# Cosine attention into a GELU feed-forward: two score passes move in front of w_in, and the norms' roots move to GpSimd

## The chip, the cores and the metric

The kernel runs on one core of a Trainium2 chip. The metric is the device time of one execution in microseconds (us). The engines of the core run side by side, each through its own queue of instructions, and wait for each other by semaphores: TensorE (PE; PEld is its weight load), VectorE (DVE), ScalarE (ACT), GpSimd (POOL) and SyncE (SP), which here only issues transfers.

## The reference

Attention over normalised q and k (8 batches, 12 heads, 448 rows, head size 64), then a feed-forward block with an exact GELU (768 to 2048 to 768).

```python
q_n = q / (np.linalg.norm(q, axis=-1, keepdims=True) + 1e-06)
k_n = k / (np.linalg.norm(k, axis=-1, keepdims=True) + 1e-06)
scores = np.matmul(q_n, k_n.transpose(0, 1, 3, 2)) / tau
attn = softmax(scores)                          # written out, with 1e-09 in the divisor
x = np.matmul(attn, v)                          # (8, 12, 448, 64), then to (3584, 768)
h = x @ w_in
g = 0.5 * h * (1.0 + erf(h / sqrt(2)))
out = g @ w_out
```

## The kernel before

Four heads make a quad; a batch has three (NQ = 3) and the kernel 24. For a quad, GpSimd squares q and k, VectorE sums the squares, a root and a reciprocal follow, GpSimd scales q and k into bf16, and a transposing transfer puts the head size on the partitions. A *pass* is the scores of one of the C = 7 chunks of keys for the four heads: four matmuls on quarter tiles (64x64) into a pair of PSUM banks (`st`), and one exponential on ScalarE that empties the pair. There are three pairs, 0 to 2, and two single banks (`mm0`, `mm1`) that everything else takes in turn. The names in the profile: `st` scores, `pt` their exponentials, `sm` row sums, `o` values, `x` normalised attention, `hp` x times w_in, `g` its GELU, `op` g times w_out, `ot` what is stored.

The norms, with the root as the exponential of half a logarithm on ScalarE (`n` counts groups of one or two quads; units 0 and 1 are the halves of quad 0, so unit u is quad u - 1 after that):

```python
groups = [[n] for n in range(NQ + 2)] + [[NQ + 2, NQ + 3]]
for n in range(2 * NQ + 1, NU, NQ):
    groups += [[n, n + 1], [n + 2]]
...
def logs(n):
    nq = nq_t.pop(n)
    ln_t[n] = nrm.tile(list(nq.shape), F32, tag="lq", name=f"lq{n}")
    nc.scalar.activation(ln_t[n], nq, AF.Ln, bias=tiny)

def roots(n):
    ...                                          # n <= NQ: another layout, same operation
        nc.scalar.activation(sr_t[n], ln, AF.Exp, scale=0.5)

def inverses(n):
    ...
        nc.gpsimd.tensor_scalar(se, sr, 1e-6, None, ALU.add)
    rn = nrm.tile(shape, F32, tag="rn", name=f"rn{n}")
    nc.vector.reciprocal(rn, se)
    rn_t[n] = rn

def root(n):
    logs(n)
    roots(n)
    inverses(n)
```

`both` is what follows the scores of a quad. `upto(f, n)` calls a step for all units below n that it was not called for yet, so it fixes where the step stands in the queues.

```python
def both(g, p):
    sums(g)          # TensorE: row sums, 16 matmuls on 128x32 tiles, in the single bank that is next
    turned(g)        # VectorE: 32x32 transposes of the sums, their sum, reciprocal, spread back
    inverted(g)
    spread(g, 0)
    spread(g, 1)
    values(g, p=p)   # TensorE: 28 matmuls on 64x64 tiles into pair p
    normalise(g, 0)  # VectorE: into x
    normalise(g, 1)
```

Attention of batch b from 1 on. `fill` holds the w_out matmuls of the batches before, 96 or 128 of them, and `run` takes the next share. After each 16th matmul of an output tile VectorE copies the single bank out to `ot`.

```python
group_pairs = [(0, 1, 2), (0, 1, 2), (0, 1, 2), (1, 2), (1, 2, 0), (1, 2, 0), (2, 0), (2, 0)]

def attention(b, fill):
    plan = {96: (20, 13, 13, 12, 16, 22), 128: (24, 18, 20, 18, 22, 26)}[len(fill)]
    ...
    g0, nu = b * NQ, (b + 1) * NQ + 1
    run()
    for n in (nu - 1, nu):
        upto(scale, n)
        upto(transposes, n)
    group(b, 1)
    upto(square, nu + 1)
    run()
    group(b, 2)
    both(g0, 0)
    upto(load_v, b + 3)
    if b == 1:
        upto(load_qk, g0 + NQ + 2)
    group(b, 3)
    upto(square, nu + 2)
    run()
    group(b, 4)
    upto(reduce, nu + 1)
    upto(load_qk, g0 + NQ + 3)
    run()
    group(b, 5)
    both(g0 + 1, 1)
    group(b, 6)
    run()
    group(b, 7)
    upto(reduce, nu + 2)
    n = 2 * b + 4
    if n < len(groups):
        logs(n)
        roots(n)
    run()
    both(g0 + 2, 1)
    if n < len(groups):
        inverses(n)
        done[root] = n + 1
```

The w_in stage: `ahead` blocks of 128 columns get the first four of their six matmuls before the last two chunks of x are there.

```python
def first(b):
    nc.scalar.preload_act_table_set(GELU_SET)
    pairs = (0, 2) if b else (0, 2, 6, 8)
    ahead = 4 if b else 5
    for m in range(ahead):
        bank(m)
        mm(m, range(KD - 2))
    ...                                          # scale, transposes, loads, square, reduce
    for m in range(ahead):
        mm(m, range(KD - 2, KD))
    for m in range(KF):
        if b == 0 and m == 8:
            for i in range(2):
                transposes(4, i)                 # on TensorE, through the single banks
                copies(4, i)
        ...                                      # matmuls of later blocks
        nc.scalar.activation(g_t[sb][:, m, hf * S:(hf + 1) * S], hps.pop(m), AF.Gelu)
        if b == 0 and m == 5:
            nc.scalar.preload_act_table_set(EXP_SET)
            upto(root, 6)
            nc.scalar.preload_act_table_set(GELU_SET)
            upto(scale, nu + 2)
            upto(transposes, nu + 2)
            upto(load_qk, 2 * NQ + 1)
    if b + 1 < B:
        nc.scalar.preload_act_table_set(EXP_SET)
        group(b + 1, 0)
        upto(root, 2 * b + 6)
```

Of the kernel before, what the change touches and what calls it, by code (L numbers as in the profile page):

```python
# [9 lines left out]
F32 = mybir.dt.float32  # L10
BF16 = mybir.dt.bfloat16
AF = mybir.ActivationFunctionType
ALU = mybir.AluOpType
# [3 lines left out]
def kernel(  # L17
# [17 lines left out]
    nc = tc.nc  # L35
    B, H, S, D = q.shape
    C = S // D
    NQ = H // 4
# [9 lines left out]
    consts = ctx.enter_context(tc.tile_pool(name="consts", bufs=1))  # L48
# [4 lines left out]
    nrm = ctx.enter_context(tc.tile_pool(name="nrm", bufs=3))  # L53
# [27 lines left out]
    nc.vector.memset(ones2[64:128, :, 1], 1.0)  # L81
    tiny = consts.tile([128, 1], F32)
    nc.vector.memset(tiny, 1e-30)
    blank = consts.tile([128, S], BF16)
    nc.vector.memset(blank, 0.0)

    root2 = [consts.tile([128, 4 * C, 2], F32, name=f"root2_{n}") for n in range(2)]
# [6 lines left out]
    EXP_SET = "natural_log_exp_and_others"  # L94
    GELU_SET = "gelu_and_others"
# [9 lines left out]
    def pair(i, name):  # L105
        pool = third[0] if i == 2 else ps_st
        return pool.tile([128, 2, 512], F32, tag=f"st{i}", name=name)
# [3 lines left out]

    units = [(0, 0, 1), (0, 1, 2)] + [(g, 0, 2) for g in range(1, NG)]
    NU = len(units)
    groups = [[n] for n in range(NQ + 2)] + [[NQ + 2, NQ + 3]]
    for n in range(2 * NQ + 1, NU, NQ):
        groups += [[n, n + 1], [n + 2]]
    shapes = [[len(gr), 2, units[gr[0]][2] - units[gr[0]][1], C] for gr in groups]
    place = {u: (n, j) for n, gr in enumerate(groups) for j, u in enumerate(gr)}
    qk_t, v_t, sq_t, nq_t, rn_t, qkb_t, qkT_t, pt_t = {}, {}, {}, {}, {}, {}, {}, {}
# [47 lines left out]
    ln_t, sr_t = {}, {}  # L167
# [5 lines that stand above are left out]

    def roots(n):
        ln = ln_t.pop(n)
        if n <= NQ:
            sr_t[n] = root2[n % len(root2)][:, :math.prod(shapes[n])]
            nc.scalar.activation(sr_t[n][:, :, 0], ln.rearrange("p j i s c -> p (j i s c)"), AF.Exp, scale=0.5)  # L178
        else:
            sr_t[n] = nrm.tile(list(ln.shape), F32, tag="sr", name=f"sr{n}")  # L180
            nc.scalar.activation(sr_t[n], ln, AF.Exp, scale=0.5)  # L181

    def inverses(n):
        sr = sr_t.pop(n)
        shape = [128] + shapes[n]
        se = nrm.tile(shape, F32, tag="se", name=f"se{n}")
        if n <= NQ:
            nc.vector.tensor_reduce(se.rearrange("p j i s c -> p (j i s c)"), sr, mybir.AxisListType.X, ALU.add)
        else:
            nc.gpsimd.tensor_scalar(se, sr, 1e-6, None, ALU.add)  # L190
        rn = nrm.tile(shape, F32, tag="rn", name=f"rn{n}")
        nc.vector.reciprocal(rn, se)  # L192
        rn_t[n] = rn

    def root(n):
        logs(n)
        roots(n)
        inverses(n)

    def scale(u, parts=None):  # L200
# [94 lines left out]
    def turned(g):  # L295
        tr = rcp.tile([128, NB, 32], F32, tag="tr", name=f"tr{g}")
        nc.vector.transpose(tr.rearrange("p b r -> p (b r)"), bank_t.pop((g, "sm"))[:, :S])  # L297
        bank_t[g, "tr"] = tr.rearrange("p b (k r) -> p k b r", k=2)
# [22 lines left out]
    def normalise(g, h):  # L321
        b, n = divmod(g, NQ)
        nc.vector.tensor_tensor(x_t[b][:, 2 * n + h, :], bank_t.pop((g, h))[:, :S], rs_t.pop((g, h)), ALU.mult)  # L323

    def both(g, p):
        sums(g)
        turned(g)
# [3 lines that stand above are left out]
        values(g, p=p)  # L331
        normalise(g, 0)
        normalise(g, 1)
# [60 lines left out]
    def upto(f, n, last=None):  # L394
        last = {load_qk: NG, load_v: NV, root: len(groups), load_wi: 4, load_wo: 4}.get(f, NU)
        while done.get(f, 0) < min(n, last):
            done[f] = done.get(f, 0) + 1
            f(done[f] - 1)
# [6 lines left out]
    def attention_first():  # L405
# [148 lines left out]
        sums(2, (6,))  # L554
        values(2, (1,))
        normalise(1, 1)
        logs(4)
        values(2, (2,))
        roots(4)
        values(2, (3,))  # L560
        turned(2)
        inverted(2)
# [9 lines left out]
        done.update({square: 6, reduce: 5, root: 5, scale: 5, transposes: 5})  # L572


    passes = [(n, c) for n in range(NQ) for c in range(C)]
    group_pairs = [(0, 1, 2), (0, 1, 2), (0, 1, 2), (1, 2), (1, 2, 0), (1, 2, 0), (2, 0), (2, 0)]

    def group(b, k):
        n0 = sum(len(p) for p in group_pairs[:k])
        for p, (n, c) in zip(group_pairs[k], passes[n0:]):  # L580
            scores(b * NQ + n, ((0, c), (1, c)), p)
            exps(b * NQ + n, ((0, c), (1, c)))

    def attention(b, fill):
        fill = list(fill)
        plan = {96: (20, 13, 13, 12, 16, 22), 128: (24, 18, 20, 18, 22, 26)}[len(fill)]
        parts = iter(plan)

        def run():
            for _ in range(next(parts)):  # L590
                fill.pop(0)()

        x_t[b] = xp.tile([128, KD, S], BF16, tag="x", name=f"x{b}")
        g0, nu = b * NQ, (b + 1) * NQ + 1
        run()
        for n in (nu - 1, nu):
            upto(scale, n)
            upto(transposes, n)
        group(b, 1)
        upto(square, nu + 1)  # L600
        run()
        group(b, 2)
        both(g0, 0)
        upto(load_v, b + 3)
        if b == 1:
            upto(load_qk, g0 + NQ + 2)
        group(b, 3)
        upto(square, nu + 2)
        run()
        group(b, 4)  # L610
        upto(reduce, nu + 1)
        upto(load_qk, g0 + NQ + 3)
        run()
        group(b, 5)
        both(g0 + 1, 1)
        group(b, 6)
        run()
        group(b, 7)
        upto(reduce, nu + 2)
        n = 2 * b + 4  # L620
        if n < len(groups):
            logs(n)
            roots(n)
        run()
        both(g0 + 2, 1)
        if n < len(groups):
            inverses(n)
            done[root] = n + 1

    def first(b):  # L630
        sb, hf = divmod(b, 2)
        if hf == 0:
            g_t[sb] = gp.tile([128, KF, 2 * S], BF16, tag="g", name=f"g{sb}")
        nc.scalar.preload_act_table_set(GELU_SET)
        nu = (b + 1) * NQ + 1
        hps = {}
        pairs = (0, 2) if b else (0, 2, 6, 8)
        ahead = 4 if b else 5

        def mm(m, kds):  # L640
            for kd in kds:
                nc.tensor.matmul(hps[m], lhsT=wi[:, kd, m * 128:(m + 1) * 128],  # L642
                                 rhs=x_t[b][:, kd, :], start=(kd == 0), stop=(kd == KD - 1))

        def bank(m):
            if m in pairs:
                p = (2, 0)[m // 2] if b else (1, 0, 1, 0)[pairs.index(m)]
                st = pair(p, f"hp{b}_{m}")
                hps[m], hps[m + 1] = st[:, 0, :S], st[:, 1, :S]
            elif m not in hps:  # L650
                hps[m] = mm_tile(f"hp{b}_{m}")[:, :S]

        for m in range(ahead):
            bank(m)
            mm(m, range(KD - 2))
        if b == 0:
            upto(square, nu + 3)
        for n in (nu + 1, nu + 2) if b else (nu + 1,):
            upto(scale, n)
            upto(transposes, n)  # L660
        if b:
            upto(load_qk, (b + 1) * NQ + 5)
        else:
            upto(load_wo, 4)
        upto(square, nu + 3)
        upto(reduce, nu + 3)
        for m in range(ahead):
            mm(m, range(KD - 2, KD))
        for m in range(KF):
            if b == 0 and m == 8:  # L670
                for i in range(2):
                    transposes(4, i)
                    copies(4, i)
            if m >= ahead and (m == 0 or m - 1 not in pairs):
                for k in range(m, m + 1 + (m in pairs)):
                    bank(k)
                    mm(k, range(KD))
            nc.scalar.activation(g_t[sb][:, m, hf * S:(hf + 1) * S], hps.pop(m), AF.Gelu)  # L678
            if b == 0 and m == 5:
                nc.scalar.preload_act_table_set(EXP_SET)  # L680
                upto(root, 6)
                nc.scalar.preload_act_table_set(GELU_SET)
                upto(scale, nu + 2)
                upto(transposes, nu + 2)
                upto(load_qk, 2 * NQ + 1)
        if b + 1 < B:
            nc.scalar.preload_act_table_set(EXP_SET)
            group(b + 1, 0)
            upto(root, 2 * b + 6)

    upto(load_qk, 1)
    nc.scalar.preload_act_table_set(EXP_SET)
# [7 lines left out]
    fill = []  # L700
    for b in range(B):
# [12 lines left out]
        fill = [f for t, ni in todo if t not in tail for f in second_pieces(sb, t, ni)]  # L714
# [38 lines left out]
```

## Time and profile before

| | us |
|---|---|
| time, median of three runs | 417.64 |
| lowest, highest | 417.42, 418.03 |
| span of the profiled execution | 416.8 |
| TensorE busy, matmuls | 409.3 |
| ScalarE busy | 246.6 |
| VectorE busy | 188.3 |
| GpSimd busy | 167.3 |

The profile is of one execution, and its times count from the start of the span. Matmuls are pipelined and their ends are modelled, so the distance of two starts says more than a printed length. The idle time before an instruction stands in brackets with what ended it. The first batch ends with its w_in stage at 52.4 us; each later one has an attention stage and then a w_in stage of 18.3 us, and the last w_out matmuls follow from 392 us.

### The profile page before, as it was taken

How to read it: one execution, taken by the hardware profiler on the slowest of the kernel's cores; microseconds unless marked ns; L12 is line 12 of the kernel's file. 1: busy time of each engine (PE TensorE's matmuls, PEld its weight loads, DVE VectorE, ACT ScalarE, POOL GpSimd, SP SyncE). 2: the span in 40 equal slices, each digit the busy share in tenths (PEclk: the TensorE clock that was granted, in tenths of full speed). 3: DMA queues.
4: the chain of work that ended last, by engine and by line, in shares of the span. 5: the costliest groups of instructions: out<-in, count | busy, mean ns of one | idle time of the engine just before them, and what ended most of it. 6: DMA issues, size and time to landing. Idle time of an engine off the chain costs nothing.

```text
span 416.8 us, 8254 instructions
## 1 busy us (share of the span) xinstructions
PE 409.3 (98%) x3506; PEld 212.1 (51%) x3506; DVE 188.3 (45%) x379; ACT 246.6 (59%) x358; POOL 167.3 (40%) x113
## 2 busy tenths in 40 slices
PE   7899999999999999999999999999999999999996
PEld 3344545555555554554555555455555554555564
DVE  5777228801676016741276314861167511661021
ACT  5995698356663578735865359735866348844300
POOL 4999706090900909053640636317280272000000
PEclk9999999999999999999999999999999999999999
DMA  8999999445473546729192382936375160430033
GB/s 288 263 259 205 204 215 258 115 81 186 91 185 77 92 174 92 187 60 242 18 233 65 77 228 43 195 77 126 141 135 180 38 90 0 85 75 2 0 77 76
DMA packets 66516, 54.53 MB, mean 131 GB/s; under 512 B 38576, under 2 KB 61488, under 8 KB 66480
## 3 DMA queue, kind: packets, MB, share of 16 engines
q1 hardware_dynamic: 53984, 41.79, 39.3%
q0 software_dynamic: 12112, 11.80, 17.8%
q8 instruction: 27, 0.44, 0.4%
q10 hardware_dynamic: 384, 0.43, 0.3%
q14 instruction: 9, 0.07, 0.1%
HBM read 45.61 MB, written 11.01 MB: 136 GB/s over the span
## 4 chain that ended last, share of the span: by engine, by line
PE 95%; DMA 2%; ACT 1%; DVE 1%; SPq 1%; issue 0%; DVEq 0%
PE hp L642 35%; PE op L352 35%; PE st L246 9%; PE o L289 8%; PE sm L275 4%; DMA qk<-in_q_dram 2%; PE op L367 1%; PE sm L266 1%; ACT pt L253 1%; SPq L129 1%; PE tp L225 0%; DVE qkT L230 0%; ACT sq L154 0%; DVE rn L192 0%; ACT root L178 0%
## 5 line engine op out<-in xcount | busy, mean ns | idle before, releaser
L253 ACT ACTIVATE pt<-st 128x896 bf16<-128x896 f32 x168 | 143.0, 917 | 39.6 <-PE st L246 38.7
L352 PE MATMUL op<-wo,g 128*128 128x384 bf16 x864 | 147.9, 327 | 0.0
L642 PE MATMUL hp<-x,wi 128*128 128x448 bf16 x768 | 146.8, 353 | 0.0
L678 ACT ACTIVATE g<-hp 128x448 bf16<-128x448 f32 x128 | 66.8, 547 | 99.3 <-PE hp L642 99.0
L352 PEld LDWEIGHTS <-g 128*128 128x128 bf16 x864 | 81.1, 98 | 63.2 <-issue 12.7
L642 PEld LDWEIGHTS <-wi 128*128 128x128 bf16 x768 | 74.4, 98 | 71.4 <-issue 2.9
L208 POOL TENSOR_TENSOR qkb<-qk,rn 128x896 bf16<-128x896 f32 (+1 forms) x49 | 79.7, 1652 | 47.1 <-DVE rn L192 47.1
L165 DVE TENSOR_REDUCE nq<-sq 128x28 f32<-128x1792 f32 (+2 forms) x30 | 48.8, 1637 | 64.6 <-POOL sq L156 61.3
L156 POOL TENSOR_TENSOR sq<-qk 128x1792 f32<-128x1792 f32 (+1 forms) x22 | 66.8, 3042 | 12.9 <-DMA qk<-in_k_dram 12.7
L356 DVE COPY ot<-op 128x384 f32<-128x384 f32 x54 | 29.5, 547 | 69.6 <-PE op L352 69.6
L190 POOL TENSOR_SCALAR se<-sr 128x28 f32<-128x28 f32 (+1 forms) x14 | 4.4, 313 | 122.7 <-ACT sr L181 122.7
L246 PE MATMUL st<-qkT 64*64 64x448 bf16 x672 | 48.3, 359 | 1.2 <-DVE qkT L230 1.0
L289 PE MATMUL o<-pt,v 64*64 64x448 bf16 x672 | 36.9, 352 | 0.0
L246 PEld LDWEIGHTS <-qkT 64*64 64x64 bf16 x672 | 18.2, 105 | 26.6 <-issue 18.3
L192 DVE RECIPROCAL rn<-se 128x28 f32<-128x28 f32 (+2 forms) x18 | 6.8, 376 | 51.4 <-POOL se L190 51.1
L318 DVE STREAM_TRANSPOSE rs<-rc 128x448 f32<-128x448 f32 x48 | 28.1, 623 | 0.8
L297 DVE STREAM_TRANSPOSE tr<-sm 128x448 f32<-128x448 f32 x24 | 15.6, 649 | 28.5 <-PE sm L275 25.4
L323 DVE TENSOR_TENSOR x<-o,rs 128x448 bf16<-128x448 f32 x48 | 27.0, 600 | 1.0 <-DVE rs L318 0.5
L289 PEld LDWEIGHTS <-v 64*64 64x64 bf16 x672 | 17.7, 106 | 15.8 <-issue 7.2
L275 PE MATMUL sm<-pt,ones 128*32 128x448 bf16 (+1 forms) x336 | 19.3, 332 | 0.0
L309 DVE TENSOR_REDUCE tr<-tr 32x28 f32<-32x28 f32 x84 | 16.5, 196 | 1.6
L275 PEld LDWEIGHTS <-ones 128*32 128x32 bf16 x336 | 7.4, 95 | 10.6 <-issue 8.9
(43 smaller groups left out, 118.5 us busy)
## 6 DMA issues: line engine op xcount, KB each, us to landing
out_dram<-ot SPq DMA_DIRECT2D x54, 192.0 KB, 2.7
qk<-in_q_dram SPq DMA_DIRECT2D x23, 448.0 KB, 6.3
qk<-in_k_dram SPq DMA_DIRECT2D x23, 448.0 KB, 7.0
v<-in_v_dram POOLq DMA_DIRECT2D x7, 672.0 KB, 10.8
wi<-in_moe_w_in_dram POOLq DMA_DIRECT2D x8, 384.0 KB, 14.3
wo<-in_moe_w_out_dram POOLq DMA_DIRECT2D x4, 768.0 KB, 14.0
qk<-in_q_dram SPq DMA_DIRECT2D x2, 224.0 KB, 3.6
v<-in_v_dram POOLq DMA_DIRECT2D x1, 448.0 KB, 9.5
```

The costliest lines, as they stand in the source:

```text
L156: eng.tensor_tensor(sq[:, part], t[:, part], t[:, part], ALU.mult)
L165: nc.vector.tensor_reduce(nq[:, part], sq[:, part], mybir.AxisListType.X, ALU.add)
L208: eng.tensor_tensor(qkb[:, i, :, s0:s1].rearrange("p c s d -> p s c d"), t[:, i, s0:s1], rn[:, i].to_broadcast([128, s1 - s0, C, D]), ALU. ...
L246: nc.tensor.matmul(st[cols, n, :S], lhsT=qkT[rows, 1, c, cols], rhs=qkT[rows, 0, :, cols], start=True, stop=True, tile_position=(64 * s, 6 ...
L253: nc.scalar.activation(pt[:, :m], st[:, :m, :S], AF.Exp, scale=inv_tau)
L275: nc.tensor.matmul(bank_t[g, "sm"][r:r + 32, cols], lhsT=ones, rhs=pt_t[g, s, c][:, cols], start=(c < 2), stop=(c >= C - 2), tile_position ...
L289: nc.tensor.matmul(bank_t[g, h][cols, :S], lhsT=v_t[g][rows, s, c, :], rhs=pt_t[g, s, c][rows], start=(c == 0), stop=(c == C - 1), tile_po ...
L318: nc.vector.transpose(rs, bank_t[g, "rc"][:, h].to_broadcast([128, NB, 32]))
L352: nc.tensor.matmul(ps[:, :NH], lhsT=g_t[sb][:, kf, t * 128:(t + 1) * 128], rhs=wo[:, kf, ni * NH:(ni + 1) * NH], start=(kf == 0), stop=(kf ...
L356: nc.vector.tensor_copy(ot[:, ni * NH:(ni + 1) * NH], ps[:, :NH])
L642: nc.tensor.matmul(hps[m], lhsT=wi[:, kd, m * 128:(m + 1) * 128], rhs=x_t[b][:, kd, :], start=(kd == 0), stop=(kd == KD - 1))
L678: nc.scalar.activation(g_t[sb][:, m, hf * S:(hf + 1) * S], hps.pop(m), AF.Gelu)
```

## The change

Two of the three score passes that followed a w_in stage now stand in front of it, behind the values of the last quad, from batch 2 on. The visits to the scores, the shares of w_out between them and the banks of the w_in stage are set anew for it. For this the first quad of the next batch must be normalised and transposed earlier, so squares, reductions and loads move too, and the groups of norms are cut differently. Roots from group 4 on are powers of one half on GpSimd, in one instruction with a tile of halves; the logarithm and the exponential on ScalarE go, and with them the two table loads in the middle of the first w_in stage. What it is for: TensorE goes from w_in straight on to w_out, without the exponentials that had to wait for the last GELU and the table load, and ScalarE has less to do between the batches.

```diff
+    halves = consts.tile([128, 8 * C], F32)
+    nc.vector.memset(halves, 0.5)
...
-    groups = [[n] for n in range(NQ + 2)] + [[NQ + 2, NQ + 3]]
-    for n in range(2 * NQ + 1, NU, NQ):
-        groups += [[n, n + 1], [n + 2]]
+    groups = [[n] for n in range(NQ + 2)] + [[NQ + 2, NQ + 3], [2 * NQ + 1]]
+    for n in range(2 * NQ + 2, NU, NQ):
+        groups += [[n], [n + 1, n + 2] if n + 2 < NU else [n + 1]]
...
         else:
+            sr = nrm.tile(shape, F32, tag="sr", name=f"sr{n}")
+            nq = nq_t.pop(n)
+            nc.gpsimd.tensor_tensor(sr, nq, halves[:, :math.prod(shapes[n])].rearrange(
+                "p (j i s c) -> p j i s c", j=shape[1], i=shape[2], s=shape[3]), ALU.pow)
             nc.gpsimd.tensor_scalar(se, sr, 1e-6, None, ALU.add)
...
     def root(n):
-        logs(n)
-        roots(n)
         inverses(n)
...
         values(2, (1,))
         normalise(1, 1)
-        logs(4)
         values(2, (2,))
-        roots(4)
...
-        plan = {96: (20, 13, 13, 12, 16, 22), 128: (24, 18, 20, 18, 22, 26)}[len(fill)]
+        plan = {96: (16, 14, 16, 18, 16, 16), 128: (20, 18, 20, 22, 32, 16)}[len(fill)]
...
-        (the body of attention as shown above)
+        g0, u = b * NQ, b * NQ + 1
         run()
+        upto(scale, u + 3)
+        upto(transposes, u + 3)
+        if b == 1:
+            upto(load_qk, g0 + NQ + 2)
+            upto(square, u + 4)
+        visit(b, (0, 1, 2))
+        if b > 1:
+            upto(scale, u + 4)
+            upto(transposes, u + 4)
         run()
+        visit(b, (0, 1, 2))
+        if b == 1:
+            upto(reduce, u + 4)
+            upto(root, 2 * b + 5)
+            upto(scale, u + 4)
+            upto(transposes, u + 4)
+        run()
+        upto(load_qk, g0 + NQ + 3)
+        visit(b, (0, 1) if b == 1 else (0, 1, 2))
+        upto(square, u + 5)
+        run()
+        visit(b, (0, 1, 2))
         both(g0, 0)
         upto(load_v, b + 3)
+        upto(load_qk, g0 + NQ + 4)
+        visit(b, (1, 2))
+        upto(reduce, u + 5)
         run()
+        visit(b, (1, 2, 0))
+        both(g0 + 1, 1)
+        visit(b, (2, 0))
+        n = 2 * b + 5
         run()
-        both(g0 + 2, 1)
+        both(g0 + 2, 2)
         if n < len(groups):
             inverses(n)
             done[root] = n + 1
+            visit(b + 1, (0, 1))
...
-        pairs = (0, 2) if b else (0, 2, 6, 8)
-        ahead = 4 if b else 5
+        pairs = {2: 0, 4: 1} if b else {0: 1, 2: 0, 6: 1, 8: 0}
+        ahead = 6 if b else 5
...
+        if b == 0:
+            (as before)
+        else:
+            upto(scale, u + 2)
+            upto(transposes, u + 2)
+            upto(load_qk, (b + 1) * NQ + 5)
+            upto(square, u + 4)
+            upto(reduce, u + 4)
...
             if b == 0 and m == 5:
-                nc.scalar.preload_act_table_set(EXP_SET)
                 upto(root, 6)
-                nc.scalar.preload_act_table_set(GELU_SET)
...
             nc.scalar.preload_act_table_set(EXP_SET)
-            group(b + 1, 0)
-            upto(root, 2 * b + 6)
+            if b == 0:
+                visit(1, (0, 1, 2))
+            else:
+                upto(root, 2 * b + 7)
```

`visit(b, pairs)` does the next passes of batch b into the pairs named. In the w_in stage `u` is the first unit of the next batch, `(b + 1) * NQ + 1`.

More of the change, by code (lines that the diff above doesn't have):

```diff
@@ L175, in roots @@
         ln = ln_t.pop(n)
[L176 to L181, printed above, removed]
+        sr_t[n] = root2[n % len(root2)][:, :math.prod(shapes[n])]
+        nc.scalar.activation(sr_t[n][:, :, 0], ln.rearrange("p j i s c -> p (j i s c)"), AF.Exp, scale=0.5)
     def inverses(n):
-        sr = sr_t.pop(n)
         shape = [128] + shapes[n]
@@ L187, in inverses @@
         if n <= NQ:
-            nc.vector.tensor_reduce(se.rearrange("p j i s c -> p (j i s c)"), sr, mybir.AxisListType.X, ALU.add)
+            nc.vector.tensor_reduce(se.rearrange("p j i s c -> p (j i s c)"), sr_t.pop(n), mybir.AxisListType.X, ALU.add)
         else:
+            sr = nrm.tile(shape, F32, tag="sr", name=f"sr{n}")
+            nq = nq_t.pop(n)
+            nc.gpsimd.tensor_tensor(sr, nq, halves[:, :math.prod(shapes[n])].rearrange(
+                "p (j i s c) -> p j i s c", j=shape[1], i=shape[2], s=shape[3]), ALU.pow)
             nc.gpsimd.tensor_scalar(se, sr, 1e-6, None, ALU.add)
@@ L575, with visit @@
     passes = [(n, c) for n in range(NQ) for c in range(C)]
[L576 to L580, printed above, removed]
+    at = {}
+    def visit(b, pairs):
+        for p in pairs:
+            n, c = passes[at.get(b, 0)]
+            at[b] = at.get(b, 0) + 1
             scores(b * NQ + n, ((0, c), (1, c)), p)
@@ L593, in attention @@
         x_t[b] = xp.tile([128, KD, S], BF16, tag="x", name=f"x{b}")
-        g0, nu = b * NQ, (b + 1) * NQ + 1
+        g0, u = b * NQ, b * NQ + 1
         run()
[L596 to L600, printed above, removed]
-        run()
-        group(b, 2)
+        upto(scale, u + 3)
[7 more added lines that the diff above has]
+            upto(transposes, u + 4)
+        run()
+        visit(b, (0, 1, 2))
[10 more added lines that the diff above has]
+        visit(b, (0, 1, 2))
         both(g0, 0)
         upto(load_v, b + 3)
[L605 to L608, printed above, removed]
+        upto(load_qk, g0 + NQ + 4)
+        visit(b, (1, 2))
+        upto(reduce, u + 5)
         run()
-        group(b, 4)
-        upto(reduce, nu + 1)
-        upto(load_qk, g0 + NQ + 3)
+        visit(b, (1, 2, 0))
+        both(g0 + 1, 1)
+        visit(b, (2, 0))
+        n = 2 * b + 5
         run()
[L614 to L624, printed above, removed]
-        both(g0 + 2, 1)
+        both(g0 + 2, 2)
         if n < len(groups):
@@ L634, in first @@
         nc.scalar.preload_act_table_set(GELU_SET)
-        nu = (b + 1) * NQ + 1
+        u = (b + 1) * NQ + 1
         hps = {}
-        pairs = (0, 2) if b else (0, 2, 6, 8)
-        ahead = 4 if b else 5
+        pairs = {2: 0, 4: 1} if b else {0: 1, 2: 0, 6: 1, 8: 0}
+        ahead = 6 if b else 5
         def mm(m, kds):
@@ L646, in bank @@
             if m in pairs:
-                p = (2, 0)[m // 2] if b else (1, 0, 1, 0)[pairs.index(m)]
-                st = pair(p, f"hp{b}_{m}")
+                st = pair(pairs[m], f"hp{b}_{m}")
                 hps[m], hps[m + 1] = st[:, 0, :S], st[:, 1, :S]
@@ L656, in first @@
         if b == 0:
[L657 to L661, printed above, removed]
+            upto(square, u + 3)
+            upto(scale, u + 1)
+            upto(transposes, u + 1)
+            upto(load_wo, 4)
+            upto(reduce, u + 3)
+        else:
+            upto(scale, u + 2)
+            upto(transposes, u + 2)
             upto(load_qk, (b + 1) * NQ + 5)
[L663 to L666, printed above, removed]
+            upto(square, u + 4)
+            upto(reduce, u + 4)
         for m in range(ahead):
@@ L679, in first @@
             if b == 0 and m == 5:
-                nc.scalar.preload_act_table_set(EXP_SET)
                 upto(root, 6)
-                nc.scalar.preload_act_table_set(GELU_SET)
-                upto(scale, nu + 2)
-                upto(transposes, nu + 2)
+                upto(scale, u + 2)
+                upto(transposes, u + 2)
                 upto(load_qk, 2 * NQ + 1)
```

## The prediction

> **What bounds the kernel now.** I read the page first: busy times, then the chain that ended last.
>
> ```profile
> PE 409.3 (98%) x3506; PEld 212.1 (51%) x3506; DVE 188.3 (45%) x379; ACT 246.6 (59%) x358; POOL 167.3 (40%) x113
> ...
> PE 95%; DMA 2%; ACT 1%; DVE 1%; SPq 1%; issue 0%; DVEq 0%
> ```
>
> TensorE is the chain, so time can come only from fewer matmuls (the change removes none), from waits inside TensorE's queue, or from gaps between kinds of matmul. These stand in TensorE's timeline, where the difference of two starts tells the true length (the printed lengths overlap). Batches 1, 3, 5 and 7 are filled with 96 matmuls of w_out, batches 2, 4 and 6 with 128. Batch 3 begins at 150.19:
>
> ```profile
> 80.55 18.33 PE L642 MATMUL hp<-x,wi 128*128 128x448 bf16 x96
> 98.82 0.76 PE L246 MATMUL st<-qkT 64*64 64x448 bf16 x12
> ...
> 150.19 0.76 PE L246 MATMUL st<-qkT 64*64 64x448 bf16 x12
> 150.88 3.42 PE L352 MATMUL op<-wo,g 128*128 128x384 bf16 x20
> 154.24 0.89 PE L246 MATMUL st<-qkT 64*64 64x448 bf16 x12
> ...
> 157.27 0.79 PE L246 MATMUL st<-qkT 64*64 64x448 bf16 x12
> 157.99 1.05 PE L275 MATMUL sm<-pt,ones 128*32 128x448 bf16 x16
> ...
> 166.56 0.85 PE L275 MATMUL sm<-pt,ones 128*32 128x448 bf16 x16
> ```
>
> Three score passes take 0.76 undisturbed and 0.89 where the third waits for the exponentials of the visit before; the row sums take 0.85, and 1.05 the first time, because the seventh pass of the quad was scored just before. A third score visit, at 163.02, shows 0.86: it waits for VectorE to free the pair of PSUM banks that held the values. At the last w_in stage the next work is w_out, not scores:
>
> ```profile
> 373.85 18.33 PE L642 MATMUL hp<-x,wi 128*128 128x448 bf16 x96
> 392.02 3.25 PE L352 MATMUL op<-wo,g 128*128 128x384 bf16 x19
> ```
>
> The same 96 matmuls took 18.17 from start to start here and 18.27 at 80.55: a change from the full array to quarter tiles costs 0.10.
>
> Then I looked for what the change moves in batch 1 (52.42 to 80.55), where the transfers are tightest. SyncE's queue, and GpSimd's and VectorE's timelines:
>
> ```profile
> 47.48 5.16 SPq L220 DMA_TRANSPOSE qkT<-qkb  x1
> 52.75 0.51 SPq L129 DMA_DIRECT2D qk<-in_q_dram  x1
> 53.31 0.47 SPq L129 DMA_DIRECT2D qk<-in_k_dram  x1
> ```
> ```profile
> 44.11 6.63 POOL L208 TENSOR_TENSOR qkb<-qk,rn 128x896 bf16<-128x896 f32 x4 [0.62 <-DVE rn L192]
> 62.00 3.17 POOL L156 TENSOR_TENSOR sq<-qk 128x1792 f32<-128x1792 f32 x1 [11.26 <-DMA qk<-in_k_dram]
> ```
> ```profile
> 59.45 0.56 DVE L356 COPY ot<-op 128x384 f32<-128x384 f32 x1 [2.96 <-PE op L352]
> ...
> 65.60 2.00 DVE L165 TENSOR_REDUCE nq<-sq 128x28 f32<-128x1792 f32 x1
> 67.52 0.55 DVE L356 COPY ot<-op 128x384 f32<-128x384 f32 x1
> ```
>
> The squares of quad 6 (batch 2's first) wait 11.26 us for its k and start at 62.00. That hurts nothing now: VectorE reaches its reduction only at 65.60, after the copy of 59.45.
>
> **What the Trainium skill says.** "TensorEngine Tiling (Array Packing)", Key Properties, says that changing the tiling mode drains TensorE; the trace agrees (the 0.10 above). "TensorE: Matmul & The Clock Gate", Architectural detail, calls VectorE and ScalarE strictly first in, first out; the timelines agree, each runs in its program's order. The same page, Part 1, says that an idle window of about 3.4 us halves TensorE's clock and a busy one restores it. The start of this trace shows the slow phase, in the matmuls of the warm-up (line by stage: length, busy and count, clock, DMA share, GB/s):
>
> ```profile
> 1.90:5.70 3.80, 3.77 (x11) 1.00 0.94 318
> 5.70:7.50 1.80, 1.80 (x11) 1.00 1.01 366
> ```
>
> Eleven took 3.8 us and then 1.8, though the granted clock reads 1.00. "GPSIMD Engine Reference", Elementwise, gives some 2.6 cycles per element for two inputs; the trace has 3.18 us for 1792 elements and 1.69 for 896, so 1.66 ns each and 0.20 fixed. No row and no page that I found tells what a power costs.
>
> **The change, part by part.**
>
> *Fewer switches.* From batch 2 on, two of the three passes behind w_in move in front of it, where values (the same quarter tiles) precede them, and the third joins other visits. Per batch w_in to scores and scores to w_out go: 19 switches become 17. Batches 2 to 7: 12 x 0.095 = 1.1 us.
>
> *Row sums.* Sums of the first quad now follow 14 passes, not 9, so the seventh's exponentials are long done: about 0.21 in each of batches 2 to 7, 1.3 us.
>
> *Score waits.* At the start of batches 3, 5, 7 no exponentials queue behind the GELU table load (1.28) any more, and 16 w_out matmuls instead of 13 stand between the values and the next score visit: 0.13 + 0.03 + 0.10 = 0.26 each, 0.8 us.
>
> Together -3.2 us. In front of w_in the two passes take pairs 0 and 1, done 0.9 and 1.7 us later; w_in reaches them after 8 and 16 matmuls, 1.5 and 3.0 us. Six blocks ahead give 24 x 0.19 = 4.5 us before the last x is needed, and VectorE's chain from sums to x is 4.4 (176.99 to 181.36). No new wait there.
>
> *ScalarE.* Per batch a logarithm and an exponential (0.34 + 0.25) twice, and two table loads in the first w_in stage (2.6 us), leave. ScalarE is not the chain: 0.
>
> *Batch 1, the new wait.* Quad 6 must now be transposed before batch 1 ends, so its reduction and reciprocal stand in VectorE's order after the second score visit and **ahead of the second w_out copy** (the one at 59.45 now). The order of loads and transposes that decides when its k lands is unchanged, so its squares still run 62.0 to 65.2. VectorE then sits in its queue: reduction to 67.25, power P, GpSimd's add 0.28, reciprocal, copy: 67.3 + P + 0.33 + 0.24 + 0.5, so the bank is free at about 68.5 + P. w_out alternates between two banks, so the fourth tile, matmul 49 of the fill, needs that copy. When is TensorE there? From 52.42: scores to 53.11, 16 matmuls (2.70) to 55.8, scores that wait as now for the table load's exponentials to 57.3 (0.65 lost, as 20 matmuls stood there before), 14 matmuls to 59.7, scores 60.35, 16 to 63.05, two scores 63.55, two matmuls: 63.9. Wait: 68.5 - 63.9 + P = **4.6 + P**. With 0.65 lost and 0.33 saved (its own row sums and score wait), batch 1 costs 4.9 + P.
>
> *P.* For 28 elements I take 1.0 us as an estimate: an add of this size takes 0.28 by the trace, and I assume a power is 10 to 20 times an add per element: 0.2 + 28 x 0.0024 x 12 = 1.0. In the first w_in stage P also stands ahead of the reciprocals that VectorE's next copies wait for; slack there is about 1 us (x ready at 36.49, needed at 37.35), and what is lost is taken off the later wait, which ends by the transfer.
>
> *Clock.* A wait of 5.6 us holds a whole idle window in about two of three phases: (5.6 - 3.4)/3.4. Recovery then loses half of 3.4 us or more, say 2.0: 1.3 on average.
>
> Sum: 417.6 - 3.2 + 4.9 + 1.0 + 1.3 = 421.6.
>
> **Rivals.** (a) *The wait does not form*: k lands some 4 us earlier, or the copy is not held. Then only the gains stand, less 0.3 in batch 1: about 414.7. For it: the w_out weights that fill the transfers end near 57, and ScalarE is freer. Against: every step ahead of that load is where it was, and the power comes before it. (b) *The power is dear* (4 us and more for 28 elements): it is paid in the first w_in stage and in batch 1, and the transposes ahead of the load of quad 6 shift with it: 426 to 430. For it: no table unit, plain cores. Against: whoever chose it kept it on a path with little slack. (c) *The clock stays up*: 420.
>
> **Range and chances.** Rival (a) has 12 in 100, (b) 12; between them P from 0.4 to 3 and the clock spread the rest over 419 to 425. So 417 to 425.5 holds eight in ten. Over 2% faster (below 409.3) is more than all gains: 1 in 100. Over 2% slower (above 426.0) is (b): 10.
>
> **What would show it.** Right: TensorE idle 4 to 7 us at about 64, released by a w_out copy; VectorE waiting for GpSimd's squares before the reduction of that batch; matmuls at double spacing just after; the first row sums at 0.85; periods of batches 2 to 7 shorter by 0.4 to 0.65. Wrong: no idle TensorE in batch 1, squares of quad 6 starting before 58, or a power of over 4 us.

## The result and the profile after

The changed kernel takes 437.53 us (436.78 to 438.44), the kernel before 417.83 beside it: a ratio of 1.047 [1.045, 1.049]. The prediction had 421.6, and 417.0 to 425.5 as its range. Busy times, the granted clock and the chain that ended last, from the page after:

```profile
PE 412.4 (95%) x3506; PEld 213.4 (49%) x3506; DVE 188.6 (43%) x381; ACT 236.7 (54%) x328; POOL 266.8 (61%) x129
...
PEclk9998969999999999999999999999999999999999
...
POOL 36%; PE 36%; DVE 12%; issue 11%; DMA 3%; ACT 0%; SPq 0%; POOLq 0%; DVEq 0%
```

TensorE was 95% of the chain, and is now 36%. GpSimd has 99.5 us more to do, and the groups of instructions, shapes apart, say with what (instructions | busy us, mean ns of one | idle before):

```profile
L189 POOL TENSOR_TENSOR sr<-nq,halves 128x56 f32<-128x56 f32 x6 | 55.9, 9315 | 11.0 <-DVE nq L167 11.0
L189 POOL TENSOR_TENSOR sr<-nq,halves 128x28 f32<-128x28 f32 x9 | 43.5, 4833 | 37.2 <-DVE nq L167 37.2
```

One power of 28 elements takes 4.83 us and one of 56 takes 9.32: (9.315 - 4.833)/28 = 0.160 us for each element, and 0.35 fixed. Where this reaches TensorE stands in its timeline, with the waits in brackets:

```profile
32.84 3.96 PE L646 MATMUL hp<-x,wi 128*128 128x448 bf16 x20
39.64 0.35 PE L646 MATMUL hp<-x,wi 128*128 128x448 bf16 x1 [2.84 <-DVE x L322]
40.17 6.95 PE L646 MATMUL hp<-x,wi 128*128 128x448 bf16 x27 [0.18 <-DVE x L322]
46.96 0.94 PE L224 MATMUL tp<-ident,qkb 128*128 128x128 bf16 x14
47.74 2.43 PE L646 MATMUL hp<-x,wi 128*128 128x448 bf16 x12
57.35 9.02 PE L646 MATMUL hp<-x,wi 128*128 128x448 bf16 x36 [7.18 <-DVE qkT L229]
66.30 0.76 PE L245 MATMUL st<-qkT 64*64 64x448 bf16 x12
...
79.69 0.48 PE L351 MATMUL op<-wo,g 128*128 128x384 bf16 x2 [1.74 <-DVE ot L355]
...
122.64 1.14 PE L351 MATMUL op<-wo,g 128*128 128x384 bf16 x6 [1.12 <-DVE ot L355]
```

Both long waits (2.84 and 7.18) name VectorE, but its timeline shows that it only passes them on: it stands in its queue before a reciprocal that waits for GpSimd. First GpSimd's timeline, then VectorE's:

```profile
32.21 4.87 POOL L189 TENSOR_TENSOR sr<-nq,halves 128x28 f32<-128x28 f32 x1
...
46.52 9.33 POOL L189 TENSOR_TENSOR sr<-nq,halves 128x56 f32<-128x56 f32 x1 [0.31 <-DVE nq L167]
```
```profile
37.50 0.33 DVE L193 RECIPROCAL rn<-se 128x28 f32<-128x28 f32 x1 [4.43 <-POOL se L191]
37.74 1.11 DVE L317 STREAM_TRANSPOSE rs<-rc 128x448 f32<-128x448 f32 x2
38.96 1.16 DVE L322 TENSOR_TENSOR x<-o,rs 128x448 bf16<-128x448 f32 x2
...
56.32 0.50 DVE L193 RECIPROCAL rn<-se 128x56 f32<-128x56 f32 x1 [9.89 <-POOL se L191]
56.74 1.08 DVE L229 COPY qkT<-tp 128x896 bf16<-128x896 bf16 x2
```

The copies at 56.74 have nothing to do with roots. They empty the two single banks that the next w_in blocks need, and stand behind the reciprocal. After these two waits TensorE runs slowly for a while; by stage (length; busy time and count of TensorE, weight loads, VectorE, ScalarE and GpSimd; granted clock, DMA share, GB/s):

```profile
33.40:36.80 3.40, 3.40 (x18) 1.66 (x17) 0.00 (x0) 0.00 (x0) 3.40 (x1) 1.00 1.17 204
40.20:46.90 6.70, 6.70 (x27) 3.05 (x27) 3.86 (x2) 2.94 (x6) 6.39 (x5) 0.75 1.27 197
57.30:66.20 8.90, 8.85 (x36) 3.97 (x35) 0.53 (x2) 2.72 (x5) 6.23 (x4) 0.76 0.54 118
```

The first row is before any wait, at clock 1.00; the others, behind the waits, read 0.75 and 0.76. The distances of starts in the two timelines give the balance, 18.6 us between the two profiled executions (spans 416.8 and 435.4):

| stage, us | before | after | difference |
|---|---|---|---|
| start, to the first w_in | 33.37 | 32.84 | -0.53 |
| first w_in stage, to the first scores of batch 1 | 33.37 to 52.42 | 32.84 to 66.30 | +14.41 |
| batch 1, to its w_in | 52.42 to 80.55 | 66.30 to 97.19 | +2.76 |
| batches 2, 4, 6, w_in to w_in, each | 51.37 | 52.35 | +0.98 |
| batches 3, 5, each | 46.40 | 46.35 | -0.05 |
| batch 7 (two passes fewer of its own) | 46.39 | 45.49 | -0.90 |
| last w_in, to the end | 42.95 | 42.96 | +0.01 |

### The profile page after: what moved, and what is told of

Same layout as the page of the kernel before. It is cut to its first block, busy times and chain, and to the rows that moved or that the text cites. A ratio compares the mean times of both kernels' runs of the same rounds, so it can differ in the third digit from the quotient of the medians.

```text
span 435.4 us, 8338 instructions
## 1 busy us (share of the span) xinstructions
PE 412.4 (95%) x3506; PEld 213.4 (49%) x3506; DVE 188.6 (43%) x381; ACT 236.7 (54%) x328; POOL 266.8 (61%) x129
## 4 chain that ended last, share of the span: by engine, by line
POOL 36%; PE 36%; DVE 12%; issue 11%; DMA 3%; ACT 0%; SPq 0%; POOLq 0%; DVEq 0%
POOL sr L189 20%; PE op L351 18%; PE hp L646 9%; POOL sq L158 9%; DVE nq L167 6%; POOL qkb L207 5%; PE st L245 4%; PE sm L274 2%; PE o L288 2%; DVE x L322 1%; PE op L366 1%; DMA qk<-in_k_dram 1%; POOL wi L380 1%; DVE tr L308 1%; DVE rs L317 1%
## 5 line engine op out<-in xcount | busy, mean ns | idle before, releaser
L646 PE MATMUL hp<-x,wi 128*128 128x448 bf16 x768 | 151.0, 358 | 10.2 <-DVE qkT L229 7.2
L189 POOL TENSOR_TENSOR sr<-nq,halves 128x28 f32<-128x28 f32 (+1 forms) x15 | 99.4, 6626 | 48.2 <-DVE nq L167 48.2
L646 PEld LDWEIGHTS <-wi 128*128 128x128 bf16 x768 | 75.4, 99 | 84.8 <-issue 18.3
L274 PE MATMUL sm<-pt,ones 128*32 128x448 bf16 (+1 forms) x336 | 17.8, 332 | 0.0
L402 PE MATMUL spin<-blank,ident 128*128 128x448 bf16 x34 | 10.0, 440 | 2.3 <-DVE root L91 2.0
```

The lines of the kernel that those rows point to most:

```text
L189: nc.gpsimd.tensor_tensor(sr, nq, halves[:, :math.prod(shapes[n])].rearrange("p (j i s c) -> p j i s c", j=shape[1], i=shape[2], s=shape[3 ...
```

## The experiments

All times are medians. Each run stands against the kernel before, measured beside it on the same chip: 418.1 us for the first four runs and 418.0 for the last four.

**The power replaced by a product** (e_mult). It leaves the square root out: the norms are half of the sums of squares. Engine, place and shape stay.

```diff
-                "p (j i s c) -> p j i s c", j=shape[1], i=shape[2], s=shape[3]), ALU.pow)
+                "p (j i s c) -> p j i s c", j=shape[1], i=shape[2], s=shape[3]), ALU.mult)
```

> The changed kernel with the power replaced by a product of the same operands, on the same engine, in the same place and shape (the norm is then half the sum of squares, so this leaves the square root out). Theory A (the time of the power alone turned the change into a loss, and the other terms of the prediction stand): with a product of about 0.25 us for 28 elements the time is 417.8 - 3.2 + 4.9 + 0.25 and up to 2.5 for the clock, 419.7 to 422.5; TensorE idle 4 to 5 us in batch 1 at about 64 us, held by a w_out copy. Rival B (having the roots in GpSimd's queue, or the new schedule, costs by itself, whatever the operation): over 428. Rival C (A, but the wait in batch 1 does not form): 414 to 416.

423.37 us, ratio 1.013 [1.012, 1.015]. Theory A, 0.9 above its span. The same instruction with another operation:

```profile
L189 POOL TENSOR_TENSOR sr<-nq,halves 128x28 f32<-128x28 f32 x9 | 2.2, 241 | 79.6 <-DVE nq L167 79.6
L189 POOL TENSOR_TENSOR sr<-nq,halves 128x56 f32<-128x56 f32 x6 | 1.8, 301 | 11.0 <-DVE nq L167 11.0
```

0.24 us against 4.83, and 14.2 of the 19.7 us lost are gone. The first w_in stage has no wait any more (19.04 us, 19.05 before). What is left is in batch 1:

```profile
63.51 0.50 PE L351 MATMUL op<-wo,g 128*128 128x384 bf16 x2
68.58 4.80 PE L351 MATMUL op<-wo,g 128*128 128x384 bf16 x16 [4.57 <-DVE ot L355]
```

This is the predicted wait at its predicted place: two matmuls into the fourth share, then 4.57 us for a w_out copy. Rivals B and C fall.

**The new schedule without powers** (e_act): logarithm and exponential on ScalarE for all groups, and the two table loads again.

```diff
-            nc.gpsimd.tensor_tensor(sr, nq, halves[...], ALU.pow)
+            lq = nrm.tile(shape, F32, tag="lq", name=f"lq{n}")
+            nc.scalar.activation(lq, nq, AF.Ln, bias=tiny)
+            nc.scalar.activation(sr, lq, AF.Exp, scale=0.5)
...
+                nc.scalar.preload_act_table_set(EXP_SET)
                 upto(root, 6)
+                nc.scalar.preload_act_table_set(GELU_SET)
```

> The changed kernel with the logarithm and the exponential back on ScalarE for all groups, with the two table loads of the first w_in stage: the new schedule of passes without the power. Theory A: 417.8 - 3.2 + 4.9 + 0.7 and up to 2.5 for the clock, 420 to 423, with the wait in batch 1; batches 2, 4, 6 shorter than before by about 0.4, 3 and 5 by about 0.6. Rival B (the schedule itself is the loss): over 428. Rival C (no wait in batch 1): 414 to 416.

422.46 us, ratio 1.012 [1.009, 1.014], theory A. First VectorE's timeline around the wait, with the line of GpSimd behind it, and TensorE's:

```profile
55.66 0.56 DVE L360 COPY ot<-op 128x384 f32<-128x384 f32 x1 [10.90 <-PE op L356]
64.72 2.02 DVE L167 TENSOR_REDUCE nq<-sq 128x28 f32<-128x1792 f32 x1 [8.50 <-POOL sq L158]
67.75 0.33 DVE L198 RECIPROCAL rn<-se 128x28 f32<-128x28 f32 x1 [1.01 <-POOL se L196]
67.99 0.95 DVE L360 COPY ot<-op 128x384 f32<-128x384 f32 x2
```
```profile
61.52 3.17 POOL L158 TENSOR_TENSOR sq<-qk 128x1792 f32<-128x1792 f32 x1 [11.04 <-DMA qk<-in_k_dram]
```
```profile
60.10 2.77 PE L356 MATMUL op<-wo,g 128*128 128x384 bf16 x16
62.80 0.57 PE L250 MATMUL st<-qkT 64*64 64x448 bf16 x8
63.31 0.50 PE L356 MATMUL op<-wo,g 128*128 128x384 bf16 x2
68.54 4.44 PE L356 MATMUL op<-wo,g 128*128 128x384 bf16 x16 [4.74 <-DVE ot L360]
72.91 0.76 PE L250 MATMUL st<-qkT 64*64 64x448 bf16 x12
```

VectorE does nothing for 8.50 us, and from about 60.4 on (two matmuls into the share of 60.10) a finished bank waits to be copied: a reduction stands ahead whose squares wait for k. Sixteen matmuls then take 4.4 us, where 16 took 2.70 before the wait. The granted clock accounts for the 1.7 us, by the same columns as above:

```profile
63.80:68.50 4.70, 0.01 (x1) 0.00 (x0) 2.77 (x4) 1.69 (x4) 1.44 (x3) 1.00 0.51 171
68.50:73.00 4.50, 4.46 (x20) 2.12 (x23) 0.45 (x1) 0.46 (x1) 4.50 (x3) 0.62 0.05 9
```

4.5 us at a mean clock of 0.62 are 1.7 lost.

**Powers from group 6 on only** (e_first): the roots of the first w_in stage (groups 4 and 5) by logarithm and exponential, with the two table loads again.

```diff
+            if n <= NQ + 2:
+                lq = nrm.tile(shape, F32, tag="lq", name=f"lq{n}")
+                nc.scalar.activation(lq, nq, AF.Ln, bias=tiny)
+                nc.scalar.activation(sr, lq, AF.Exp, scale=0.5)
+            else:
+                (the power, as changed)
```

> The changed kernel with logarithm and exponential for groups 4 and 5 alone (the roots that the first w_in stage waits for, with their two table loads); powers from group 6 on. Theory A with a power of 4.8 us: the first w_in stage ends at about 52.4 as before, and the wait in batch 1 forms and holds the power: 417.8 - 3.2 + 4.9 + 4.8 + 2 for the clock + 1.3 in each of batches 2, 4, 6 and 0.5 in 3 and 5, about 431. Rival D (the first w_in stage is the whole loss, and the power is hidden later on): 415 to 419.

432.32 us, ratio 1.035 [1.033, 1.037], theory A. The first w_in stage is as long as before (32.38 to 51.42, 19.04 us), and the wait of batch 1 now carries a power:

```profile
62.70 0.50 PE L356 MATMUL op<-wo,g 128*128 128x384 bf16 x2
72.84 2.40 PE L356 MATMUL op<-wo,g 128*128 128x384 bf16 x7 [9.64 <-DVE ot L360]
```

The wait is 4.9 longer than in e_act: the reciprocal comes 7.34 us after the start of the reduction and not 3.03, so 4.3 later, and TensorE is there 0.6 earlier. So the delays do not add up. In the changed kernel the first w_in stage loses 14.4 us, and the transfer of k goes on meanwhile: the squares that wait for it start 2.1 us after the first scores of batch 1 (68.36 and 66.30), here 10.1 (61.50 and 51.42). Only 1.74 us of the wait are left there.

**Powers in the kernel before** (e_pow_only): schedule and groups stay.

```diff
     def logs(n):
+        if n > NQ:
+            return
     (roots likewise)
     def inverses(n):
+        (for n > NQ the power of the changed kernel)
...
-                nc.scalar.preload_act_table_set(EXP_SET)
                 upto(root, 6)
-                nc.scalar.preload_act_table_set(GELU_SET)
```

> The kernel before with the power in place of logarithm and exponential from group 4 on, and without the two table loads; the schedule of passes stays. Theory A: the first w_in stage gets longer by about 14 us (two waits of 3.5 and 7.3 and the clock), and nothing later waits: about 432. Rival E (each batch pays the power of 9.3 us on its way from attention to w_in): over 440.

433.23 us, ratio 1.037 [1.035, 1.040], theory A: TensorE waits 2.84 and 7.19 us in the first w_in stage, and for no other power later. Six powers of 56 elements and six of 28 after that stage cost about 0.1 us a batch (51.48 and 46.53 from w_in to w_in, 51.37 and 46.40 before). Those of 56 run beside w_in (the first from 90.38 to 99.70, with w_in from 94.48 to 112.74). Those of 28 run just behind it, from 112.74 to 117.57, and the w_out copy that follows the reciprocal, at 118.22, is still in time: TensorE needs its bank at about 119.5, an estimate from the starts and the shares.

**The order in VectorE's queue** (e_late): e_act, and in batch 1 the reduction of quad 6 behind the second w_out copy.

```diff
         run()
         visit(b, (0, 1, 2))
-        if b == 1:
-            upto(reduce, u + 4)
-            upto(root, 2 * b + 5)
-            upto(scale, u + 4)
-            upto(transposes, u + 4)
         run()
         upto(load_qk, g0 + NQ + 3)
         visit(b, (0, 1) if b == 1 else (0, 1, 2))
+        if b == 1:
+            upto(reduce, u + 4)
-        upto(square, u + 5)
+        else:
+            upto(square, u + 5)
         run()
         visit(b, (0, 1, 2))
+        if b == 1:
+            sqrts(2 * b + 4)                     # logarithm and exponential
-        both(g0, 0)
+        both(g0, 0, (lambda: upto(root, 2 * b + 5)) if b == 1 else None)   # behind inverted
+        if b == 1:
+            upto(scale, u + 4)
+            upto(transposes, u + 4)
+            upto(square, u + 5)
...
         visit(b, (1, 2))
-        upto(reduce, u + 5)
+        if b > 1:
+            upto(reduce, u + 5)
...
         visit(b, (2, 0))
+        upto(reduce, u + 5)
```

> The new schedule without powers (logarithm and exponential on ScalarE), and in batch 1 the reduction of quad 6 one visit later (behind the second w_out copy), its roots behind the exponentials of the fourth visit, its reciprocal inside the first normalisation, and the squares and the reduction of quad 7 behind that. Theory A (the order in VectorE's queue is the cause of the wait of 4.9 in batch 1): the wait goes, TensorE has no gap over 0.4 there but the one of 0.8 for the exponentials of the first visit, and the time is 417.8 - 3.2 + 0.3 = 415, 414 to 416. Rival F (the transfers are the cause, and the wait only moves to a later instruction): 418 to 423.

415.95 us, ratio 0.995 [0.992, 0.997], theory A. VectorE's and TensorE's timelines:

```profile
60.81 0.56 DVE L369 COPY ot<-op 128x384 f32<-128x384 f32 x1 [4.41 <-PE op L365]
64.77 2.02 DVE L167 TENSOR_REDUCE nq<-sq 128x28 f32<-128x1792 f32 x1 [3.40 <-POOL sq L158]
```
```profile
63.49 3.10 PE L365 MATMUL op<-wo,g 128*128 128x384 bf16 x18
66.52 0.76 PE L257 MATMUL st<-qkT 64*64 64x448 bf16 x12
67.31 0.85 PE L286 MATMUL sm<-pt,ones 128*32 128x448 bf16 x16
```

The squares come as late as ever (the reduction begins at 64.77, not 64.72), but the copy now lies before them, and the fourth share runs through in 3.0 us. The transfer was a condition of the wait; the order was its cause, and rival F falls. The steps of quad 7 that the run moves as well lie behind the wait (its squares start at 71.52 in e_act). Batch 1 still takes 29.26 us up to its w_in, 1.1 more than before, where 0.3 was expected; 0.4 of it is two passes that batch 7 has no longer.

**Shares of w_out in batch 1** (e_late20): e_late and

```diff
+        if b == 1:
+            plan = (20, 13, 13, 18, 16, 16)
```

> The kernel of the run before, and in batch 1 the shares of w_out 20, 13, 13, 18, 16, 16 in place of 16, 14, 16, 18, 16, 16. Theory A: the gap of 0.8 at the second visit of batch 1 shrinks to about 0.3, 0.65 us less than without it. Rival: the wait only moves to the next visit, same time.

415.98 us, ratio 0.995 [0.994, 0.997]: the rival is right. From start to start, the second visit takes 0.81 instead of 1.46, but the third takes 0.97 instead of 0.70, and the first row sums wait for a w_out copy:

```profile
67.74 0.85 PE L286 MATMUL sm<-pt,ones 128*32 128x448 bf16 x16 [1.24 <-DVE ot L369]
```

That copy stands behind the same late reduction, which begins no sooner (65.20, and 64.77 in e_late). That TensorE is there sooner does not make the transfer of k end sooner; TensorE only waits longer.

**A power where there is slack** (e_latepow): e_late with powers for groups 7, 9, ... 17.

```diff
-    POWERS = ()
+    POWERS = range(7, 19, 2)
```

> e_late with the power on GpSimd for the groups of one quad at the end of each attention stage (7, 9, ... 17: 28 elements, 4.8 us each). Theory A (a power costs time only where an instruction that TensorE needs stands behind it, and here VectorE still has the normalisation ahead of the reciprocal): same as e_late within 0.5 us. Rival E (every power is paid): 6 x 4.8 less some slack, over 425.

416.17 us, ratio 0.995 [0.993, 0.997]: theory A, 0.2 from e_late. One of the six, in GpSimd's timeline and then VectorE's:

```profile
124.02 4.84 POOL L191 TENSOR_TENSOR sr<-nq,halves 128x28 f32<-128x28 f32 x1 [9.02 <-DVE nq L167]
128.94 0.29 POOL L203 TENSOR_SCALAR se<-sr 128x28 f32<-128x28 f32 x1
```
```profile
134.89 1.12 DVE L334 TENSOR_TENSOR x<-o,rs 128x448 bf16<-128x448 f32 x2
135.93 0.31 DVE L205 RECIPROCAL rn<-se 128x28 f32<-128x28 f32 x1
```

The sum is ready 6.7 us before VectorE gets to the reciprocal. With or without these six powers the time is the same.

**Powers for all groups from 7 on** (e_lateall): `POWERS = range(7, 19)`.

> e_late with powers for all groups from 7 on, so also for those of two quads at the end of each w_in stage (9.3 us). Theory A: the reciprocal ahead of the first w_out copies is late again: 1.3 us in each of batches 2, 4, 6 and 0.5 in each of 3, 5 (as in the changed kernel, gaps of 1.45 and 0.65 where 0.16 is normal), so e_late plus 4.8. Rival: w_in hides it, same as e_late.

424.43 us, ratio 1.015 [1.011, 1.018]: the direction of theory A, and 8.5 us over e_late in place of 4.8. Batches 3 to 6 lose what was expected (0.6 and 1.4 in turn). Batch 2 loses 6.0 in the profiled execution, where 1.3 was expected:

```profile
108.98 2.08 PE L365 MATMUL op<-wo,g 128*128 128x384 bf16 x6 [2.86 <-DVE ot L369]
```

2.86 us, where 1.12 had been idle in the changed kernel: here quad 7 is squared and reduced later in batch 1, so each step to the power of 9.3 us comes later too (it begins 16.4 us after the start of w_in, and 14.7 in the changed kernel). Behind the wait stands a slow spell, six matmuls in 2.0 us: the granted clock is 0.50 from 108.1 to 115.0, and TensorE, back at 108.98, loses half of 6.0 us. Not every execution has it: this one took 426.33 us at a mean clock of 0.992, two others 423.45 and 424.18 at 1.000. Without the spell these two are still 7.5 and 8.2 us over e_late.

## Why the prediction was wrong

**The step that failed is P.** "For 28 elements I take 1.0 us as an estimate ... I assume a power is 10 to 20 times an add per element": it measured 4.83, or 0.160 us per element against the 0.029 assumed, so 67 times the 0.0024 of an add. The estimate came from an add because no row had a power, so it was a guess in the shape of a sum. The product in the same place takes 0.24 and takes back 14.2 us; e_act, without powers, is 15.1 below the changed kernel. The prediction's own sign of being wrong, a power of over 4 us, is what the profile shows.

**The overlap that rested on P failed with it.** Put into the sum, 4.83 gives 425.4; the other 12 us are in places for which the sum had no term.

- *The first w_in stage, 14.4 us.* The prediction saw that P stands ahead of VectorE's copies there ("slack there is about 1 us") and counted nothing. By its own rate that holds, as an estimate: the powers of 28 and 56 elements would be 3.9 and 7.5 us shorter than the measured 4.87 and 9.33, more than the waits of 2.84 and 7.18. With the real power the waits were 2.8 + 0.2 + 7.2 us, and the clock took the rest, about 4. "What is lost is taken off the later wait" held: the wait in batch 1 shrank from 9.64 (e_first) to 1.74.
- *The powers of 56 elements behind the later w_in stages.* They hold a w_out copy for 1.1 us in batches 2, 4 and 6 and for 0.3 in 3 and 5. Against e_act these batches are 1.4 and 0.6 longer, where the gains were 0.42 and 0.66.

Rival (b), "the power is dear", was what happened, in the main by this path; it got 12 in 100, and even its 426 to 430 was short, as it did not work the first w_in stage through.

**The wait in batch 1 was right, where nothing is lost before it.** 4.6 + P was the figure; with P = 0.24 it was 4.57, with logarithm and exponential 4.74, with a power 9.64. In the changed kernel itself 1.74 was left. The reason given, a reduction that waits for late squares ahead of the second copy, is shown by e_late.

**The clock was right in size and wrong in its condition.** 1.7 us after the wait of 4.74, where a slow spell of about 2.0 was expected. But it was given two chances in three, and in all eight executions of e_mult and e_act the mean clock is below 1 (0.991 to 0.996); and waits shorter than the idle window of the prediction were followed by slow spells too (last section).

**The gains were right.** -3.2 was predicted for batches 2 to 7. In e_late these run from the w_in at 81.60 to that at 371.28, 289.7 us against 293.3 before (80.55 to 373.85), 3.6 less, of which 0.4 is two passes that batch 1 took over: -3.2. In e_act the batches are 0.42 and 0.66 shorter in turn, with 0.4 to 0.65 predicted, so the sum is not luck. The first row sums take 0.85. ScalarE's 10 us less brought nothing: e_mult, with 236.5 us on ScalarE, is not faster than e_act with 246.7.

## What to carry to other kernels

Before an operation moves to another engine, find a line of a profile with its duration there; where there is none, measure that one instruction, and do not scale it from an add. Then ask what stands behind it in each queue that waits for it: here a power of 4.8 us was free where VectorE came to the reciprocal later anyway (e_latepow), and cost nearly its whole length where a copy that TensorE needed stood behind the reciprocal (e_first). In this kernel an instruction that waits for a transfer belongs behind the copies that free PSUM, even when its own result is urgent (e_late).

## What was unexpected of the hardware

A power on GpSimd costs 0.160 us per element of each partition, some 20 times a product of the same shape at 28 elements and 31 times at 56 (9.32 against 0.30 in e_mult).

And TensorE slowed after less idle time than the prediction's window. After 2.84 and 0.18 us in the first w_in stage it ran at a mean granted clock of 0.75 from 40.2 to 46.9: 1.00 up to 41.0, then 0.50 for 3.4 us. In e_lateall the clock fell to 0.50 within a wait of 2.86, 2.0 us after its beginning, and stayed there for 6.9 us, in some of the executions only. After 1.74 us in batch 1 of the changed kernel no slow spell showed. What decides between these cases was not tested.
